# Values of a woven block in three visits to the banks instead of four, and two blocks' stores issued later from six output tiles

## Chip, cores and metric

The kernel runs on one core of one Trainium2 chip. Its metric is the device time of one execution in microseconds (us). A core has a matmul engine (TensorE, in profile rows PE, its weight loads PEld), VectorE (DVE), ScalarE (ACT), GpSimd (POOL) and SyncE (SP), which only issues transfers. Each takes its instructions in program order and waits at an instruction until the semaphores that it needs are there.

## What is computed

Attention inside chunks of 64 tokens, then a feed-forward layer with a squared ReLU:

```python
# q, k, v: (8, 8, 576, 64), chunks of 64
scores = scale * np.matmul(q_c, k_c.transpose(0, 1, 2, 4, 3))
attn = np.exp(scores) / np.sum(np.exp(scores), axis=-1, keepdims=True)
out = np.matmul(attn, v_c)
# x: (4608, 512), w_in: (512, 2048), w_out: (2048, 512)
h = np.maximum(x @ w_in, 0.0)
return (h * h @ w_out).astype(np.float32)
```

(The reference also subtracts each row's maximum before the exponential and adds 1e-9 to the sum.)

## The kernel before

The 4608 tokens are 18 groups of 256 (four chunks each), and 9 blocks of two groups. Groups 14 and 15, which are block 7, are put together from the last chunk of every batch entry ("rest"); their loads take more and smaller transfers.

**Attention of a group.** q and k are loaded by SP, cast to bf16 (`C`, lines 283 and 286, on GpSimd or ScalarE) and transposed by SP as a DMA (`TD`, line 292; the first groups by PE). `scores` (PE, line 315) writes 32 matmuls of 64x64 to a PSUM tile of two banks, `ps_att`; ScalarE takes the exponential into a tile `e` (line 326). `values` (PE, line 342) multiplies `e` with v. v has a column of ones, so each head pair's output of 64 columns has the row sum as its 65th. For each of the two token tiles `t` of a group there is one visit to the bank: 4 head pairs x 4 = 16 matmuls of 65 columns. After a visit `out_of_x` has VectorE take the reciprocals of the sums (line 276) and multiply (line 277) into a tile `x`. `transpose_x` (`XT`) turns `x` into `xT`, in the woven part from block 5 on by an SP DMA (line 366).

**Feed-forward.** Blocks 0 to 3 go through `ffn_in` (line 410) and then their output product. From block 4 on, both products are done in seven part products each in place of eight, by sums of quarters. The x sums (`x_sums`, on VectorE through line 444) have to be there before a block's first product (line 487, `quad_product`). Outputs are summed into tiles `o_sb` and stored by GpSimd (`store`, line 635).

**The woven part.** From block 4 on the order is written by hand. Each block `j` has 16 slots; in each there stand in-products of block `j` (`quad_step`), a piece of the output products of block `j - 1` (line 606), and what `at(j, slot, ...)` puts there. A slot such as 3.5 stands after the in-products of slot 4 and before its output products. For the attention of block `j + 1`:

```python
S0, V0, V1, X0 = ((1.5, 3.5), (4.5, 7.5), (6, 9.5), (10.5, 11)) if j == QUADS else (
    (0.5, 7), (2,8), (3.5, 9.5), (3.5, 11.5)) if is_whole(blocks[j + 1][0]) else (
    (3.5, 9), (5, 10), (7, 11.5), (11.5, 12))
```

These are the slots of scores (S0), of the first and second value visit (V0, V1) and of `XT` (X0), for the block's two groups. The first line is for block 5, the second for blocks 6 and 8, the third for block 7. All of these visits use the one `ps_att` tile, so each waits until the reader of the visit before is done. The loads of block `j + 2` are issued by SP in the same slots, one per slot, or two where that block is the "rest".

**Stores.** `summed_out` adds into an `o_sb` and calls `defer`, which in blocks 1 and 2 issues the store at once and later 8 slots later (`after`; `tock` counts the slots). The casts of groups 6 and 7 stand in GpSimd's queue between block 1's first and second store.

Of the kernel before, what the change touches and what calls it, by code (L numbers as in the profile page):

```python
# [11 lines left out]
FP32 = mybir.dt.float32  # L12
# [6 lines left out]
def kernel(  # L19
# [197 lines left out]
    def att_bank():  # L217
        if "out" in banks:
            return ps_att.tile([128, 1024], FP32, name="ps_att")
        state["att"] = state.get("att", 0) + 1  # L220
        if state["att"] % 2:
            return ps_att.tile([128, 1024], FP32, name="ps_att")
        return ps_att2.tile([128, 1024], FP32, name="ps_att2")
# [19 lines left out]
            copy(out=dst[:, t], in_=src[:, t])  # L243

    def qkT_tile():
        return att_pool.tile([128, 2, 2, n_hp, 128], BF16, name="qkT", bufs=4)

    def transpose_qk(g, q_pool, k_pool):
        if ("qkT", g) not in state:
# [18 lines left out]

    def e_tile():
        return att_pool.tile([128, 1024], BF16, name="e", bufs=3)  # L270

    def out_of_x(x, ps, n):

        o = ps[:, :, 0:n * (D + 1)].rearrange("p a (h d) -> p a h d", d=D + 1)
        rec = att_pool.tile([128, 2, n], FP32, name="rec", bufs=4)
        nc.vector.reciprocal(out=rec, in_=o[:, :, :, D])
        nc.vector.tensor_tensor(  # L277
            out=x, in0=o[:, :, :, 0:D], in1=rec.to_broadcast([128, 2, n, D]), op=ALU.mult)

    def cast_qk(g, copies):  # L280
        qkb = att_pool.tile([128, 2, 2 * H * D], BF16, name="qkb", bufs=2)
# [43 lines left out]
            s_in = ps.rearrange("p (b i q) -> p b q i", i=2, q=CH // 2)  # L325
        nc.scalar.activation(out=e_out, in_=s_in, func=AF.Exp, scale=scale)  # L326

    def values(g, tiles=(0, 1)):
        e = state["e", g]
        veb = v_even[g % NV].bitcast(BF16)  # L330
        vob = [v_odd[odd_tile[g, c] % NO].bitcast(BF16) for c in range(4)]
        if 0 in tiles:
            state["x", g] = att_pool.tile([128, 2, n_hp, 2, D], BF16, name="x", bufs=3)
        x = state["x", g]
        for t in tiles:
            ps = att_bank().rearrange("p (a f) -> p a f", a=2)
            for hp in range(n_hp):
                for a in range(2):
                    for p in range(2):
                        c = p ^ a  # L340
                        vb = vob[2 * t + p] if a else veb[:, t]
                        nc.tensor.matmul(  # L342
                            out=ps[64 * p:64 * p + 64, a, hp * (D + 1):(hp + 1) * (D + 1)],
                            lhsT=e[64 * c:64 * c + 64, a, hp, t, :],
                            rhs=vb[64 * c:64 * c + 64, hp, 1::2],
                            start=True, stop=True)
            out_of_x(x[:, t].rearrange("p h a d -> p a h d"), ps, n_hp)

    def transpose_x_early(g, t):
        psb = ps_ffn.tile([128, 512], FP32, name="ps_ffn").bitcast(BF16)  # L350
# [122 lines left out]
    def after(n, f):  # L473
        later.append((state["clock"] + n, f))
# [83 lines left out]
    def ffn_out(j):  # L558
# [82 lines left out]
                    in_=o_sb[:, t * HD:(t + 1) * HD])  # L641

        def o_tile():
            return ffn_pool.tile([128, n_tt * HD], FP32, name="o_sb", bufs=4)

        def summed_out(name, s, half, col):
            o = o_tile()
# [2 lines left out]
            defer(lambda: store(nc.gpsimd, o, half, col))  # L650

        def defer(f):
            if "out" in banks:
                    after(8, f)
            else:
                f()

        A, BC = 0, 1
        s1 = kept()
# [56 lines left out]
    def ffn_out_by_ft(j):  # L716

        n_tt = BT // 128
        o_ps = [ps_ffn.tile([128, d_model], FP32, name="ps_ffn") for _ in range(n_tt)]

        def mm(tt, ft):
            nc.tensor.matmul(  # L722
                out=o_ps[tt],
                lhsT=g_piece(j, tt // 2, ft // HF, ft % HF // 4)[
                    :, ft % 4, tt % 2 * 128:tt % 2 * 128 + 128],
                rhs=w_out_bf[:, ft, :],
                start=(ft == 0), stop=(ft == n_ft - 1))


        for ft in range(n_ft - 4):  # L730
            for tt in range(n_tt - 1 if ft == 0 else n_tt):
                mm(tt, ft)
                if ft == 1 and tt == n_tt - 2:
                    mm(n_tt - 1, 0)
            yield
        for tt in range(n_tt):
            for ft in range(n_ft - 4, n_ft):
                mm(tt, ft)
            o_sb = ffn_pool.tile([128, d_model], FP32, name="o_sb", bufs=4)
            nc.scalar.copy(out=o_sb, in_=o_ps[tt])  # L740
            b, s0 = chunks[blocks[j][tt // 2]][0]
            t0 = b * S + s0 + tt % 2 * 128
            nc.gpsimd.dma_start(out=out[t0:t0 + 128, :], in_=o_sb)
            yield
# [6 lines left out]
        for g in grps:  # L751
            yield from v_pieces(g)

    SC, AV, XT = scores, values, transpose_x
    TD = transpose_qk_dma

    def TE(g):
# [17 lines left out]
            copies = nc.gpsimd.tensor_copy, nc.gpsimd.tensor_copy  # L775
        cast_qk(g, copies)

    def AV0(g):
        values(g, [0])

    def AV1(g):
        values(g, [1])

    HT = BT // 2
    go(pieces([0, 1]))
# [37 lines left out]
    for j in range(QUADS):  # L823
        grps, nxt, far = blocks[j], blocks[j + 1], blocks[j + 2]
        plan = {}

        def at(slot, f, *x):
            plan.setdefault(slot, []).append((f, x))

        if j == 0:  # L830
            loads, go_slots = pieces(far), range(17)
            at(28, summed(b11_p_b21, b11, b21))
            for slot, f in ((24, TA), (27, SC), (29, AV), (31, XT)):
                at(slot, f, nxt[0])
            at(31, TQ, nxt[1])
            at(31, summed(b22_m_b21, b22, b21, ALU.subtract))
            phases = [first_ffn_in, ffn_out_by_ft(0)]
        elif j == 1:
            loads, go_slots = itertools.chain(*map(qk_pieces, far)), range(26, 48)
            for slot, f in ((1, TK), (4, SC), (7, AV), (12, XT)):  # L840
                at(slot, f, grps[1])
            for i, g in enumerate(nxt):
                for slot, f in ((16 + 4 * i, C), (21 + 4 * i, TD), (36 + i, SC), (38 + 2 * i, AV),
                                (41 + 2 * i, XT)):
                    at(slot, f, g)
            for i, g in enumerate(far):
                at(36 + 4 * i, C, g)
                at(42 + 3 * i, TD, g)
            at(2, summed(b12_p_b21, b12, b21))
            at(12, summed(b11_m_b12, b11, b12, ALU.subtract))  # L850
            at(20, summed(b12_p_b22, b12, b22))
            out_j = ffn_out(1)
            for i in (20, 27, 29, 31):
                at(i, lambda: next(out_j)())
            phases = [ffn_in(1, [(0, 256, FT_ORDER), (256, 256, FT_ORDER)]), out_j]
        else:
            out_j = ffn_out(j)
            for i in (14, 15):
                at(i, lambda: next(out_j)())
            phases = [ffn_in(j, [(0, BT, range(n_ft))])]  # L860
            if j == 2:
                loads, go_slots = itertools.chain(*map(v_pieces, nxt), pieces(far)), [
                    *range(16), *range(27, 36)]
                slots = {SC: (8, 7), AV: (10, 12), XT: (11, 14), C: (21, 26), TD: (29, 29)}
                for f in (C, TD):
                    for i, g in enumerate(far):
                        at(slots[f][i], f, g)
                phases.append(out_j)
            else:
                loads, go_slots = pieces(far), range(16)  # L870
                slots = {SC: (2, 4), AV: (7, 13), XT: (14, 15)}
            for f in (SC, AV, XT):
                for i, g in enumerate(nxt):
                    at(slots[f][i], f, g)
            if j == 2:
                for i, f in enumerate((summed(a21_p_a22, a21, a22),
                                       summed(a12_m_a21, a12, a21, ALU.subtract),
                                       summed(a11_p_a21, a11, a21))):
                    at(1 + 2 * i, f)
        slot = 0  # L880
        for phase in phases:
            for _ in phase:
                if slot in go_slots:
                    for f in loads:
                        f()
                        break
                for f, x in plan.get(slot, []):
                    f(*x)
                slot += 1
        assert all(x < slot for x in plan), (j, slot, sorted(plan))  # L890
        if j < QUADS - 1:
            go(loads)
# [19 lines left out]
    for j in range(QUADS, n_blk):  # L912
# [25 lines left out]
            plan.setdefault(("out", 16 * (j - QUADS) + s), []).append(outs[j - 1])  # L938

        if j + 1 < n_blk:  # L940
            S0, V0, V1, X0 = ((1.5, 3.5), (4.5, 7.5), (6, 9.5), (10.5, 11)) if j == QUADS else (
                (0.5, 7), (2,8), (3.5, 9.5), (3.5, 11.5)) if is_whole(blocks[j + 1][0]) else (
                (3.5, 9), (5, 10), (7, 11.5), (11.5, 12))
            for i, g in enumerate(blocks[j + 1]):
                at(j, S0[i], SC, g)
                at(j, V0[i], AV0, g)
                at(j, V1[i], AV1, g)
                at(j, X0[i], XT, g)
            for i, s in enumerate((13.5, 15, 17.5, 18)):
                at(j, s, x_sums, j + 1, i)  # L950
# [65 lines left out]
```

## Time and profile before

| | us |
|---|---|
| median of 3 runs | 287.72 |
| the runs | 284.68, 287.72, 289.44 |
| the profiled execution, device time | 285.11 |
| its span from first to last instruction | 283.2 |
| mean granted TensorE clock in it | 0.997 |

The page of the profile gives busy time by engine, the costliest groups of instructions, and the chain of work that ended last: from the last instruction back, at each step to what released it. Rows of a group give its line, engine, operation and tiles, its count, then busy time and the mean of one in ns. Some that matter here:

```profile
L410 PE MATMUL ps_ffn<-xT,w_in_bf 128*128 128x512 bf16 (+1 forms) x328 | 58.7, 333 | 0.3 <-DVE xT L376 0.2
L487 PE MATMUL ps_ffn<-qk_st,w_in_bf 128*128 128x256 bf16 x240 | 35.4, 273 | 1.8 <-DVE qk_st L444 1.7
L277 DVE TENSOR_TENSOR x<-ps_att,rec 128x512 bf16<-128x512 f32 x36 | 24.9, 692 | 1.2
L326 ACT ACTIVATE e<-ps_att 128x1024 bf16<-128x1024 f32 x18 | 18.4, 1024 | 12.7 <-PE ps_att L315 12.7
out_dram<-o_sb POOLq DMA_DIRECT2D x31, 256.0 KB, 3.9
```

The mean of one matmul is its time in the pipeline, of which several lie over one another; what a matmul takes of PE is the distance to the next one's start. The last row is a group of transfers: issued by GpSimd, 31 times, at most 256 KB each, 3.9 us from issue to landing in the median. By stretches, the DMA engines are busy throughout until about 211 us (a share near 1), then loads end.

### The profile page before, as it was taken

What the parts mean: (1) busy time and instruction counts of PE and PEld (TensorE: products, weight loads), DVE (VectorE), ACT (ScalarE), POOL (GpSimd) and SP (SyncE); (2) the same over time, 40 slices, a digit from 0 to 9 for tenths busy, and PEclk for the clock granted to TensorE, in tenths of its full rate; (3) what the DMA queues carried; (4) which work ended last, traced back from release to release, by engine and by line L of the source; (5) the groups of instructions that cost most, each with busy time, mean ns of one, the idle gap of its engine ahead of it and who ended that gap; (6) DMA issues with size and microseconds to landing.
All of it is one profiled execution on the core that took longest, in us unless ns stands there. A gap on an engine that the chain in (4) does not pass through costs nothing.

```text
span 283.2 us, 7888 instructions
## 1 busy us (share of the span) xinstructions
PE 266.0 (94%) x3255; PEld 202.9 (72%) x3258; DVE 199.2 (70%) x360; ACT 162.5 (57%) x292; POOL 92.6 (33%) x123
## 2 busy tenths in 40 slices
PE   1999999999998999997999999899999999999994
PEld 1774454778773468445888788688888888888783
DVE  1266615899648592388989998489879877984842
ACT  1537705786446764875666775476657664656330
POOL 2037834150242002132025425432543322431612
PEclk9999999999999999999999999999999999999998
DMA  7999999999998999999999899599996320120312
GB/s 199 239 299 362 374 331 248 317 215 178 264 218 231 234 212 237 269 247 195 271 241 189 224 197 223 121 254 258 229 180 175 74 73 6 80 71 0 93 58 111
DMA packets 139699, 56.61 MB, mean 200 GB/s; under 512 B 108496, under 2 KB 135376, under 8 KB 139664
## 3 DMA queue, kind: packets, MB, share of 16 engines
q1 hardware_dynamic: 136656, 46.81, 75.4%
q0 software_dynamic: 2864, 9.18, 9.5%
q8 instruction: 25, 0.41, 0.6%
q10 hardware_dynamic: 144, 0.13, 0.1%
q14 instruction: 10, 0.08, 0.1%
HBM read 36.70 MB, written 9.44 MB: 163 GB/s over the span
## 4 chain that ended last, share of the span: by engine, by line
PE 78%; DMA 9%; DVE 7%; ACT 2%; issue 1%; POOL 0%; SPq 0%; DVEq 0%; ACTq 0%
PE ps_ffn L487 20%; PE ps_out L606 19%; PE ps_ffn L410 14%; PE ps_ffn L606 11%; PE ps_ffn L722 5%; DMA qk_st<-in_k_dram 4%; DMA xT<-x 3%; PE ps_att L315 3%; DMA qkT<-qkb 2%; PE ps_att L342 2%; DVE x L277 2%; DVE gT L428 2%; PE ps_ffn L267 1%; PE ps_ffn L234 1%; DVE relu L495 1%
## 5 line engine op out<-in xcount | busy, mean ns | idle before, releaser
L410 PE MATMUL ps_ffn<-xT,w_in_bf 128*128 128x512 bf16 (+1 forms) x328 | 58.7, 333 | 0.3 <-DVE xT L376 0.2
L606 PEld LDWEIGHTS <-w_st 128*128 128x128 bf16 x512 | 49.2, 98 | 7.9 <-DVE w_st L444 1.2
L428 DVE TENSOR_TENSOR gT<-relu 128x256 bf16<-128x256 bf16 (+2 forms) x69 | 34.8, 532 | 21.4 <-ACT relu L421 21.0
L495 DVE CUSTOM_DVE_ANT_0 relu<-ps_ffn,w_st 128x512 f32<-128x512 f32 x60 | 39.2, 684 | 13.2 <-PE ps_ffn L487 11.9
L421 ACT ACTIVATE relu<-ps_ffn 128x256 bf16<-128x256 f32 (+2 forms) x82 | 39.8, 503 | 13.0 <-PE ps_ffn L410 11.7
L410 PEld LDWEIGHTS <-w_in_bf 128*128 128x128 bf16 x328 | 30.8, 98 | 21.6 <-DVE xT L376 0.4
L487 PE MATMUL ps_ffn<-qk_st,w_in_bf 128*128 128x256 bf16 x240 | 35.4, 273 | 1.8 <-DVE qk_st L444 1.7
L635 POOL DMA_DIRECT2D out_dram<-o_sb x27 | 19.8, 732 | 50.3 <-DVE o_sb L444 49.4
L487 PEld LDWEIGHTS <-w_in_bf 128*128 128x128 bf16 x320 | 30.5, 98 | 6.3 <-DVE qk_st L444 2.6
L606 PEld LDWEIGHTS <-gT 128*128 128x128 bf16 x296 | 28.6, 98 | 3.6
L606 PE MATMUL ps_out<-w_out_bf,w_st 128*128 128x256 bf16 x240 | 30.8, 273 | 0.0
L529 ACT ACTIVATE w_st<-ps_ffn 128x512 f32<-128x512 f32 x20 | 11.9, 596 | 28.4 <-PE ps_ffn L487 28.4
L277 DVE TENSOR_TENSOR x<-ps_att,rec 128x512 bf16<-128x512 f32 x36 | 24.9, 692 | 1.2
L326 ACT ACTIVATE e<-ps_att 128x1024 bf16<-128x1024 f32 x18 | 18.4, 1024 | 12.7 <-PE ps_att L315 12.7
L487 PEld LDWEIGHTS <-qk_st 128*128 128x128 bf16 x240 | 22.7, 98 | 2.9
L506 POOL TENSOR_TENSOR qk_st<-relu 128x512 bf16<-128x512 f32 x10 | 10.3, 1034 | 43.3 <-DVE relu L495 43.3
L487 PE MATMUL ps_ffn<-xT,qk_st 128*128 128x256 bf16 x160 | 23.9, 273 | 0.0
L506 POOL TENSOR_TENSOR gT<-relu 128x512 bf16<-128x512 f32 x10 | 10.3, 1033 | 38.0 <-DVE relu L495 38.0
L283 POOL CAST qkb<-qk_st 128x1024 bf16<-128x1024 f32 x12 | 13.3, 1104 | 18.6 <-DMA qk_st<-in_q_dram 10.3
L606 PE MATMUL ps_ffn<-w_out_bf,w_st 128*128 128x256 bf16 x144 | 17.7, 273 | 0.4 <-DVE w_st L444 0.3
L504 ACT ACTIVATE gT<-relu 128x512 bf16<-128x512 f32 x28 | 17.7, 632 | 0.0
L444 DVE TENSOR_TENSOR w_st<-gT,w_st 128x1024 bf16<-128x1024 bf16 x26 | 17.0, 687 | 0.0
(83 smaller groups left out, 419.9 us busy)
## 6 DMA issues: line engine op xcount, KB each, us to landing
qk_st<-in_q_dram SPq DMA_DIRECT2D x16, 512.0 KB, 5.8
out_dram<-o_sb POOLq DMA_DIRECT2D x31, 256.0 KB, 3.9
qk_st<-in_k_dram SPq DMA_DIRECT2D x24, 256.0 KB, 5.6
ve_sb<-in_v_dram SPq DMA_DIRECT2D x32, 128.0 KB, 4.4
w_st<-in_moe_w_in_dram SPq DMA_DIRECT2D x8, 512.0 KB, 6.6
w_st<-in_moe_w_out_dram SPq DMA_DIRECT2D x8, 512.0 KB, 6.2
vo_sb<-in_v_dram SPq DMA_DIRECT2D x24, 128.0 KB, 4.1
qk_st<-in_k_dram SPq DMA_DIRECT2D x4, 512.0 KB, 6.7
```

The costliest lines, as they stand in the source:

```text
L277: nc.vector.tensor_tensor(out=x, in0=o[:, :, :, 0:D], in1=rec.to_broadcast([128, 2, n, D]), op=ALU.mult)
L326: nc.scalar.activation(out=e_out, in_=s_in, func=AF.Exp, scale=scale)
L410: nc.tensor.matmul(out=h[:, 0:n], lhsT=w_in_bf[:, dt, ft * 128:(ft + 1) * 128], rhs=xT[:, c // 128:(c + n) // 128, dt, :], start=(dt == 0) ...
L421: nc.scalar.activation(out=rl[:, 0:n], in_=h[:, 0:n], func=AF.Relu)
L428: nc.vector.tensor_tensor(out=dst, in0=src, in1=src, op=ALU.mult)
L444: nc.vector.tensor_tensor(out=out, in0=in0, in1=in1, op=op)
L487: nc.tensor.matmul(out=bank[:, f * GT:(f + 1) * GT], lhsT=a[:, dt, ft * 128:(ft + 1) * 128], rhs=b[:, :, dt, :], start=(first and f == 0 a ...
L495: nc.vector._custom_dve(TENSOR_ADD_SAT, out=out, in0=in0, in1=in1, s0=BIG, s1=0.0)
L504: engine.activation(out=dst, in_=r, func=AF.Square)
L506: engine.tensor_tensor(out=dst, in0=r, in1=r, op=ALU.mult)
L606: nc.tensor.matmul(out=out_ps, lhsT=lhsT, rhs=b[:, i, :], start=(first and i == 0 and (last or t == 0)), stop=(i == HF - 1), skip_group_ch ...
L635: dma.dma_start(out=out[t0:t0 + GT, col:col + HD].rearrange("(t p) d -> p t d", p=128), in_=o_sb.rearrange("p (t d) -> p t d", d=HD))
```

## The change

A visit no longer holds one token tile of one group. `values` takes a list of parts (group, tile, head pair), up to seven, whose columns (7 x 65 = 455 of a bank's 512) fit one bank on each side. The 16 parts of a block's two groups are cut into visits of 7, 7 and 2 (`AVB`). The second visit spans both groups, so it has two multiplies, one of 1 part and one of 6. In blocks 0 to 3 and the start a visit is one tile as before (`AV`). The slots of the woven part change with it. `qkT` has three buffers in place of four, `o_sb` six in place of four. The stores of block 1 are issued 12 slots later, those of block 2 ten; the slots of blocks 0 to 3 are counted for it.

```diff
-        return att_pool.tile([128, 2, 2, n_hp, 128], BF16, name="qkT", bufs=4)
+        return att_pool.tile([128, 2, 2, n_hp, 128], BF16, name="qkT", bufs=3)
...
-    def values(g, tiles=(0, 1)):
...
+    def values(parts):
+
+        ps = att_bank().rearrange("p (a f) -> p a f", a=2)
+        for n, (g, t, hp) in enumerate(parts):
+            if (t, hp) == (0, 0):
+                state["x", g] = att_pool.tile([128, 2, n_hp, 2, D], BF16, name="x", bufs=3)
+            e = state["e", g]
+            veb = v_even[g % NV].bitcast(BF16)
+            for a in range(2):
+                for p in range(2):
+                    c = p ^ a
+                    vb = v_odd[odd_tile[g, 2 * t + p] % NO].bitcast(BF16) if a else veb[:, t]
+                    nc.tensor.matmul(
+                        out=ps[64 * p:64 * p + 64, a, n * (D + 1):(n + 1) * (D + 1)],
+                        lhsT=e[64 * c:64 * c + 64, a, hp, t, :],
+                        rhs=vb[64 * c:64 * c + 64, hp, 1::2],
+                        start=True, stop=True)
+        o = ps[:, :, 0:len(parts) * (D + 1)].rearrange("p a (h d) -> p a h d", d=D + 1)
+        rec = att_pool.tile([128, 2, 7], FP32, name="rec", bufs=4)[:, :, 0:len(parts)]
+        nc.vector.reciprocal(out=rec, in_=o[:, :, :, D])
+        for g in sorted({z[0] for z in parts}):
+            n = [i for i, z in enumerate(parts) if z[0] == g]
+            n0, n1 = n[0], n[-1] + 1
+            u = n_hp * parts[n0][1] + parts[n0][2]
+            nc.vector.tensor_tensor(
+                out=state["x", g].rearrange("p t h a d -> p a (t h) d")[:, :, u:u + n1 - n0],
+                in0=o[:, :, n0:n1, 0:D],
+                in1=rec[:, :, n0:n1].to_broadcast([128, 2, n1 - n0, D]), op=ALU.mult)
...
-            return ffn_pool.tile([128, n_tt * HD], FP32, name="o_sb", bufs=4)
+            return ffn_pool.tile([128, n_tt * HD], FP32, name="o_sb", bufs=6)
...
         def defer(f):
-            if "out" in banks:
-                    after(8, f)
-            else:
-                f()
+            after((12, 10)[j - 1] if j < 3 else 8, f)
...
+    def AVB(j, i):
+        cuts = (0, 7, 14, 16)
+        both = [z for g in blocks[j] for z in parts_of(g)]
+        values(both[cuts[i]:cuts[i + 1]])
...
                 slot += 1
+                tock()
...
-            S0, V0, V1, X0 = ((1.5, 3.5), (4.5, 7.5), (6, 9.5), (10.5, 11)) if j == QUADS else (
-                (0.5, 7), (2,8), (3.5, 9.5), (3.5, 11.5)) if is_whole(blocks[j + 1][0]) else (
-                (3.5, 9), (5, 10), (7, 11.5), (11.5, 12))
+            S0, V0, X0 = ((1.5, 3.5), (6, 7.5, 9.5), (10.5, 11)) if j == QUADS else (
+                (0.5, 2.5), (4.5, 8, 9.5), (9, 11.5)) if is_whole(blocks[j + 1][0]) else (
+                (3.5, 5.5), (8, 10, 11.5), (11.5, 12))
             for i, g in enumerate(blocks[j + 1]):
                 at(j, S0[i], SC, g)
-                at(j, V0[i], AV0, g)
-                at(j, V1[i], AV1, g)
+            for i in range(3):
+                at(j, V0[i], AVB, j + 1, i)
+            for i, g in enumerate(blocks[j + 1]):
                 at(j, X0[i], XT, g)
```

More of the change, by code (lines that the diff above doesn't have):

```diff
@@ L270, in e_tile @@
         return att_pool.tile([128, 1024], BF16, name="e", bufs=3)
[L272 to L278, printed above, removed]
     def cast_qk(g, copies):
@@ L326, in scores @@
         nc.scalar.activation(out=e_out, in_=s_in, func=AF.Exp, scale=scale)
-    def values(g, tiles=(0, 1)):
[L329 to L347, printed above, removed]
+    def values(parts):
[25 more added lines that the diff above has]
+                in1=rec[:, :, n0:n1].to_broadcast([128, 2, n1 - n0, D]), op=ALU.mult)
@@ L349, in transpose_x_early, with parts_of @@
+    def parts_of(g, tiles=(0, 1)):
+        return [(g, t, hp) for t in tiles for hp in range(n_hp)]
     def transpose_x_early(g, t):
@@ L738, in ffn_out_by_ft @@
                 mm(tt, ft)
-            o_sb = ffn_pool.tile([128, d_model], FP32, name="o_sb", bufs=4)
+            o_sb = ffn_pool.tile([128, d_model], FP32, name="o_sb", bufs=6)
             nc.scalar.copy(out=o_sb, in_=o_ps[tt])
@@ L752, in pieces @@
             yield from v_pieces(g)
-    SC, AV, XT = scores, values, transpose_x
+    SC, XT = scores, transpose_x
     TD = transpose_qk_dma
@@ L776, in C, with AV @@
         cast_qk(g, copies)
[L778 to L782, printed above, removed]
+    def AV(g, tiles=(0, 1)):
+        for t in tiles:
+            values(parts_of(g, [t]))
+    def AVB(j, i):
+        cuts = (0, 7, 14, 16)
+        both = [z for g in blocks[j] for z in parts_of(g)]
+        values(both[cuts[i]:cuts[i + 1]])
     HT = BT // 2
```

## The prediction

> **What bounds the kernel now.** I read the page's busy line and chain first:
>
> ```profile
> PE 266.0 (94%) x3255; PEld 202.9 (72%) x3258; DVE 199.2 (70%) x360; ACT 162.5 (57%) x292; POOL 92.6 (33%) x123
> PE 78%; DMA 9%; DVE 7%; ACT 2%; issue 1%; POOL 0%; SPq 0%; DVEq 0%; ACTq 0%
> ```
>
> TensorE bounds it: only 17.2 us of the 283.2 us span are not PE time, and some 11 us of these lie in the start (0 to 20 us, 6.5) and the tail (after 266 us, 4.3), which the change does not touch. So the next view is one of windows, for the four stretches in which attention of the next block is woven in; two of them:
>
> ```profile
> 156.00:183.50 27.50, 26.17 (x344) 22.06 (x344) 22.71 (x42) 17.44 (x31) 12.15 (x13) 1.00 0.89 191
> 210.90:238.00 27.10, 27.09 (x355) 23.15 (x356) 22.65 (x41) 17.02 (x30) 6.94 (x8) 1.00 0.40 99
> ```
>
> The columns are the length, then PE, weight load, DVE, ACT and POOL busy, granted clock, DMA share, GB/s. The second stretch is full of matmuls; the first has 1.33 us without one. Where, the chain of waits in order of time says (start, length, what):
>
> ```profile
> 84.81 6.41 DMA qkT<-qkb
> 91.26 0.45 PE ps_att L315 x32
> ...
> 179.87 3.19 DMA xT<-x
> 183.08 0.44 DVE qk_st L444
> 183.56 1.05 PE ps_ffn L487 x8
> ...
> 205.58 0.69 DVE x L277
> 206.30 4.10 DMA xT<-x
> 210.91 1.05 PE ps_ffn L487 x8
> ```
>
> Three times PE stands for a DMA transpose: at 91.26 for the scores of group 7, and at 183.56 and 210.91 for the first product of blocks 6 and 7, whose x sums (DVE, L444) wait for xT. A chain row of 8 matmuls of 256 columns takes 0.87 us, 0.109 each. The last matmuls before 183.56 are 8 from 181.13 on, so PE was free at 182.00 and stood 1.56; before 210.91 the same count gives 0.46. Those are the waits that a PE saving can run into.
>
> **Fewer visits.** What a visit of the values to the bank costs, the PE timeline shows:
>
> ```profile
> 143.76 1.04 PE L606 MATMUL ps_out<-w_out_bf,w_st 128*128 128x256 bf16 x8
> 144.73 0.22 PE L342 MATMUL ps_att<-ve_sb,e 64*64 64x65 bf16 x2
> ...
> 144.99 0.72 PE L487 MATMUL ps_ffn<-qk_st,w_in_bf 128*128 128x256 bf16 x5
> ```
>
> 143.76 + 8 x 0.109 = 144.63, and the visit begins at 144.73: 0.095 to get in. Its 16 small matmuls start within about 0.13 us and the next large one comes at 144.99, some 0.095 more than their own spacing. So 0.19 us of each visit is entry and exit; the matmuls (about 10 ns each) stay the same. Four woven blocks go from 16 visits to 12: 4 x 0.19 = 0.75 us off PE, if nothing else waits.
>
> On DVE the four reciprocals (L276, 198 ns) become three, and four multiplies of 512 elements (L277, 692 ns) become four of 896, 128, 768 and 256. Taking the 198 ns of the tiny one as the fixed part, an element costs (692 - 198)/504, about 1 ns: 1.08, 0.31, 0.95 and 0.44 us, together as before. But the first two visits hold the bank longer: 0.2 + 1.08 = 1.3 us and 0.2 + 0.31 + 0.95 = 1.46, against 0.9. The tightest place is block 5's, where 12 matmuls (1.31 us) stand between the first and the second visit: results at about 144.85, multiply done at 146.2, second visit due at 146.16. I put 0.1 us there, bounds 0 and 0.6 (one more DVE instruction queued ahead). The other gaps hold 20 to 52 matmuls (2.2 us or more): nothing, or 0.3 with the same instruction ahead.
>
> **Scores earlier.** For blocks 6 and 8 the second group's scores move from slot 7 to 2.5, for block 7 from 9 to 5.5. Their input comes by an SP transpose (L292). For group 13:
>
> ```profile
> L292 SPq DMA_TRANSPOSE qkT<-qkb x1: 2715/2715/2715, 156.9 to 156.9; - x1
> ...
> DMA to landing us min/median/max: 6.3/6.3/6.3
> ```
>
> It lands at 156.87 + 6.3 = 163.2. In the new order these scores follow 8 output products (from 159.99) and 4 matmuls: 159.99 + 12 x 0.109 + 0.09 = 161.4. PE will stand 1.8 us there, a wait that before does not have, with everything of PE behind it. What is late next? PE reaches the start of block 6 at 182.00 + 1.8 - 0.19 - 0.19 (two visits saved) = 183.4, and that start is set by the transpose anyway: 179.87 + 3.19 + 0.46 = 183.5. So the new wait takes the place of the old one and costs about 0.0, provided that the second xT transpose of block 6 still issues at 179.87. On SP, the first one moves behind ten loads (slot 3.5 to 9); the loads are the same, so the second stays where it is if the first need not wait at its new place. The ten loads were issued from 167.80 to 175.3; without the transpose ahead, which ran from 166.28, SP is through with them at about 173.7. The x is done after the second visit (170.02 before, so about 171.8, plus 0.5 and the reciprocal and short multiply, 0.5 to 0.9): 172.8 to 173.2. Half a microsecond of margin.
>
> For block 8 the group's transpose (issued 211.49, 4.2 to landing) is there at 215.7 and its scores are due 20 matmuls behind the first group's (213.63 + 0.38 + 2.18 + 0.09, less 0.4 from the next part: 215.9): nothing, bounds 0 and 0.3. For block 7, the transpose issued at 185.75 has landed long before 193: nothing.
>
> **Block 7's x.** Its last visit now holds 2 of 16 parts: 0.25 us less multiply, 0.08 less on PE, 0.23 us earlier by the visit already saved, less some delay of the longer multiply ahead. I take x 0.4 us earlier (bounds 0 and 0.75), so the 206.30 transpose and the 210.91 start move 0.4: that is what block 7's saving of 0.19 and its wait of 0.46 allow.
>
> **Stores and tiles.** Eight stores are issued 12 or 10 slots later in the program, but in GpSimd's queue only one changes its place: block 1's first, which passes the casts of groups 6 and 7. The other seven have the same neighbours and the same semaphore to wait for.
>
> ```profile
> 73.71 0.71 POOL L635 DMA_DIRECT2D out_dram<-o_sb  x1 [9.42 <-DVE o_sb L444]
> 84.72 2.14 POOL L635 DMA_DIRECT2D out_dram<-o_sb  x3
> ```
>
> So x1 and x3 become x4 from 84.72. The casts between them waited for loads (1.1 to 2.1 us each), not for the store. The page's queue 0 has 2864 packets, 9.18 MB and 9.5% of 16 engines' span: 3.2 KB and 150 ns a packet. So a store of 256 KB is 80 packets, about 0.8 us of the 16 engines. Without it the loads of group 7 may land up to 0.8 us earlier, with it the transpose at 84.81 may land 0.8 later: ends -0.8 and +0.8 at the wait before 91.26, and I take 0, as the traffic only moves. qkT with three buffers: a transpose waits for scores three groups back, which are over a block old; nothing. Six output tiles: nothing waited for one.
>
> **Sum.** Start of block 6: 0 (-0.1 to +0.4), and what blocks 5 and 6 saved is gone in it. Block 7: -0.4. Block 8: -0.19, with 0 for its scores. Stores 0. Together -0.6; on the profiled execution's own time of 285.11 (span 283.2 and 1.9 around it) that is 284.5. The other runs gave 284.68, 287.72 and 289.44; the median of the four is 286.4, and 286.4 - 0.6 = 285.8.
>
> **Rivals.**
> - *The scores' wait is not absorbed* (slower). If x of group 12 is later than SP's arrival at 173.7, SP stands, and every load and the second transpose behind it slip by as much; a slip of 1.56 keeps the old wait as well. Price 1.8 - 0.19 = 1.6 at block 6, in all +1.0: 286.1 profiled, 287.4 beside the runs. For it: the margin is only 0.5. Against: it must be overrun by 1.5 to count fully. 0.2.
> - *The fourth store delays the transpose* (slower). With three stores in flight the transpose at 84.81 took 6.4 us, the one for group 13, with one (issued 156.79), 6.3, so rows do not settle it. Price 0.8 at 91.26, in all +0.2: 285.3 profiled, 286.6 beside the runs. The Trainium skill, "DMA: Bandwidth & Descriptors", section "SWDGE vs HWDGE vs iDMA", says that DMAs from GpSimd and from SP sit in different queues of each engine, which it serves in turn; by it a fourth store takes its share from the transpose. 0.12.
> - *More is won.* Group 7's loads land 0.8 earlier, the transpose too, and SP carries that through to 183.5: -0.6 - 0.8 = -1.4, at most -2.3 (0.75 of visits, 1.1 that PE waits for the transpose before 91.26, 0.46 before 210.91): 282.8 to 283.7 profiled. 0.13.
> - *It does nothing*, PE's saving being taken up by DMA everywhere: 0, 285.1. That lies within 0.6 of the forecast and shares its chance of 0.5; 0.05 is left for what I do not see.
>
> **Numbers.** The likeliest is 285.8. The range goes from the fastest time shown less 1.8, inside the larger gain (282.9), to the slowest less 0.4, inside the forecast and the second rival (289.0); the runs' own scatter of 4.8 us is most of it. A change under 2% (5.8 us) cannot be told from none here, and no case above reaches it; what I leave beyond is for unseen causes and scatter: faster 0.1, same 0.83, slower 0.07.
>
> **What would show it.** Right: 12 value visits after 136 us; a wait of 1.5 to 2 us before L315's scores near 161, and none or little before block 6's first product at 183.4 to 183.7; four stores in a row from about 84; the 210.91 start a little earlier relative to 183.5. Wrong: a gap before a value visit of more than 0.5 us, both waits (161 and 183) present, or the transpose before 91 landing much later. The sum would be overturned if the loads' pace on SP changed, since they, not PE, set the start of block 6.

## The result, and the profile after

The changed kernel takes 296.44 us in the median of six runs (295.03 to 298.07), the kernel before 287.39 in the runs beside it (284.68 to 294.36). The ratio is 1.034, with a 95% interval of 1.028 to 1.041: slower by some 9 us. The ratios here and below leave out runs over 1.5% above the fastest of the same kernel, so they differ a little from the quotients of the medians. The forecast was 285.8, with a range up to 289.0. The profiled execution took 296.31 us, its span 294.4, at a mean granted TensorE clock of 0.979 (before 0.997).

The busy line and the chain's shares, from the page of the changed kernel:

```profile
PE 270.2 (92%) x3258; PEld 205.2 (70%) x3258; DVE 197.6 (67%) x356; ACT 163.2 (55%) x292; POOL 93.1 (32%) x123
PE 67%; DMA 12%; DVE 8%; SPq 7%; ACT 3%; issue 1%; POOL 1%; ACTq 0%
```

The span grew by 11.2 us and PE's busy time by 4.2 only, although PE has fewer visits to make. So most of the time was not lost on PE's own work (and a part of the 4.2 is the half clock, see below). The chain says SPq 7% where it said 0%, and DMA 12% where it said 9%; that is a hint and no more, for the chain splits differently from one execution to the next. What PE waits for, by line, releaser, total, times and longest (us), first before:

```profile
PE ps_att L371 <- DVE x L277: 2.1, 2, 1.6
PE ps_ffn L487 <- DVE qk_st L444: 1.7, 2, 1.4
PE ps_att L315 <- DMA qkT<-qkb: 1.1, 1, 1.1
```

and after (L307 is the scores, L374 the PE transposes of `x`, L490 the first products):

```profile
PE ps_att L307 <- DMA qkT<-qkb: 7.0, 3, 3.5
PE ps_att L374 <- DVE x L344: 2.5, 1, 2.5
PE ps_ffn L490 <- DVE qk_st L447: 1.2, 2, 1.1
```

The row that grew is the scores' wait for the DMA transposes of q and k, 1.1 to 7.0 us. Two of them in the chain of waits, in order of time:

```profile
85.88 8.12 DMA qkT<-qkb
94.05 0.45 PE ps_att L307 x32
...
163.74 7.84 DMA qkT<-qkb
171.62 0.45 PE ps_att L307 x32
```

The first is the transpose for group 7, which before was issued at 84.81 and took 6.41; the second is the one for group 13, before 6.3 us from 156.9. Both start later and take longer. And PE pays for its waits a second time, by the view of windows (length, then PE, weight load, DVE, ACT and POOL busy, granted clock, DMA share, GB/s):

```profile
72.00:100.00 28.00, 24.49 (x365) 15.14 (x364) 14.11 (x29) 15.00 (x22) 6.96 (x8) 0.94 1.04 222
94.40:97.81 3.41, 3.41 (x51) 1.38 (x40) 0.43 (x1) 2.48 (x3) 0.00 (x0) 0.50 1.07 220
135.40:138.81 3.41, 3.41 (x22) 2.22 (x19) 1.53 (x3) 1.76 (x3) 0.22 (x1) 0.50 0.82 180
156.00:183.50 27.50, 23.82 (x312) 19.65 (x312) 22.42 (x40) 15.41 (x28) 10.68 (x12) 0.94 1.00 191
172.90:176.31 3.41, 3.41 (x44) 2.24 (x42) 2.88 (x5) 1.26 (x3) 1.73 (x2) 0.50 1.08 204
183.50:211.00 27.50, 27.50 (x338) 23.90 (x337) 22.06 (x39) 17.57 (x32) 12.67 (x15) 1.00 0.86 197
```

Directly behind the wait that ends at 94.05 the clock is granted at half for 3.41 us; so it is from 135.4 and from 172.9, behind waits of 2.6 and 3.7 us. None of this was in the windows of before, all at 1.00 between 60 and 238 us.

How far the same matmul is later than before, at points of the order that both kernels share, worked out from the two traces: 0.4 us at 62, 1.2 at 74, 4.2 at 93.4 (a wait of 2.93 where it was 1.23, and the half clock), 6.5 at 132 (a wait of 2.64 where it was 1.81, and the half clock), 11.5 at 168 (a wait of 3.66 before group 13's scores, new, and the half clock), 10.0 at the start of block 6, 11.1 at 224. The growth ends where the loads end. (A wait is here, as in the prediction, the distance between the starts of two matmuls less the spacing of the first; the views count from its modelled end and give 0.16 to 0.17 us less.)

The row of the `qkT` transposes themselves, first before, then after (SP's issue of one in ns, least, median and most; then from issue to landing):

```profile
L292 SPq DMA_TRANSPOSE qkT<-qkb x14: 1617/2020/3817, 65.8 to 211.5; - x14
DMA to landing us min/median/max: 3.8/4.4/6.4
```

```profile
L284 SPq DMA_TRANSPOSE qkT<-qkb x14: 1328/2852/4108, 67.0 to 222.5; - x14
DMA to landing us min/median/max: 4.3/4.9/8.1
```

The change issues the same 14 transposes of the same size in the same places, and yet the median issue went from 2.02 to 2.85 us and even the quickest landing from 3.8 to 4.3. Queueing would move the median and the worst; a least time that rises points at the transfer itself. The sum of the 14 issues is 32.6 us before and 38.9 after. While SP issues a transpose it issues none of the loads behind it.

### The profile page after: what moved, and what is told of

Same layout as the page of the kernel before. It is cut to its first block, busy times and chain, and to the rows that moved or that the text cites. A ratio compares the mean times of both kernels' runs of the same rounds, so it can differ in the third digit from the quotient of the medians.

```text
span 294.4 us, 7869 instructions
## 1 busy us (share of the span) xinstructions
PE 270.2 (92%) x3258; PEld 205.2 (70%) x3258; DVE 197.6 (67%) x356; ACT 163.2 (55%) x292; POOL 93.1 (32%) x123
## 4 chain that ended last, share of the span: by engine, by line
PE 67%; DMA 12%; DVE 8%; SPq 7%; ACT 3%; issue 1%; POOL 1%; ACTq 0%
PE ps_out L609 19%; PE ps_ffn L490 19%; PE ps_ffn L413 11%; PE ps_ffn L609 9%; DMA qkT<-qkb 5%; PE ps_ffn L722 5%; DVE gT L431 4%; DMA w_st<-in_moe_w_in_dram 3%; DMA qk_st<-in_k_dram 2%; SPq L136 2%; PE ps_att L332 2%; PE ps_att L307 2%; SPq L181 2%; DMA xT<-x 2%; SPq L177 1%
## 5 line engine op out<-in xcount | busy, mean ns | idle before, releaser
L413 PE MATMUL ps_ffn<-xT,w_in_bf 128*128 128x512 bf16 (+1 forms) x328 | 61.3, 341 | 1.0 <-POOL w_in_bf L197 0.6
L431 DVE TENSOR_TENSOR gT<-relu 128x256 bf16<-128x256 bf16 (+2 forms) x69 | 34.2, 525 | 25.9 <-ACT relu L424 25.2
L413 PEld LDWEIGHTS <-w_in_bf 128*128 128x128 bf16 x328 | 31.1, 99 | 23.9 <-issue 1.8
L490 PE MATMUL ps_ffn<-qk_st,w_in_bf 128*128 128x256 bf16 x240 | 35.6, 273 | 1.2 <-DVE qk_st L447 1.2
L490 PEld LDWEIGHTS <-w_in_bf 128*128 128x128 bf16 x320 | 31.1, 98 | 5.6 <-DVE qk_st L447 1.8
L609 PE MATMUL ps_out<-w_out_bf,w_st 128*128 128x256 bf16 x240 | 31.4, 276 | 0.0
L344 DVE TENSOR_TENSOR x<-ps_att,rec 128x512 bf16<-128x512 f32 (+4 forms) x36 | 24.5, 690 | 1.1
L490 PEld LDWEIGHTS <-qk_st 128*128 128x128 bf16 x240 | 23.1, 98 | 2.9
L490 PE MATMUL ps_ffn<-xT,qk_st 128*128 128x256 bf16 x160 | 24.0, 276 | 0.0
```

Source lines behind the costliest of these rows:

```text
L344: nc.vector.tensor_tensor(out=state["x", g].rearrange("p t h a d -> p a (t h) d")[:, :, u:u + n1 - n0], in0=o[:, :, n0:n1, 0:D], in1=rec[: ...
L413: nc.tensor.matmul(out=h[:, 0:n], lhsT=w_in_bf[:, dt, ft * 128:(ft + 1) * 128], rhs=xT[:, c // 128:(c + n) // 128, dt, :], start=(dt == 0) ...
L431: nc.vector.tensor_tensor(out=dst, in0=src, in1=src, op=ALU.mult)
L490: nc.tensor.matmul(out=bank[:, f * GT:(f + 1) * GT], lhsT=a[:, dt, ft * 128:(ft + 1) * 128], rhs=b[:, :, dt, :], start=(first and f == 0 a ...
L609: nc.tensor.matmul(out=out_ps, lhsT=lhsT, rhs=b[:, i, :], start=(first and i == 0 and (last or t == 0)), stop=(i == HF - 1), skip_group_ch ...
```

## The experiments

Each was run beside the kernel before on the same chip; ratios are to it, with 95% intervals. The first four split the change as the prediction had seen it.

**Scores back to their slot.** The changed kernel, with the second scores of blocks 6 and 8 where they were:

```diff
-                (0.5, 2.5), (4.5, 8, 9.5), (9, 11.5)) if is_whole(blocks[j + 1][0]) else (
+                (0.5, 7), (4.5, 8, 9.5), (9, 11.5)) if is_whole(blocks[j + 1][0]) else (
```

> The changed kernel with one thing put back: the second group's scores of blocks 6 and 8 stand at slot 7 again, as before, not at 2.5. Theory S (these scores now stand ahead of the landing of their transpose; PE idles 3.66 us at 171.6, which also brings 3.41 us at half clock, and 0.95 at 227.6; 1.5 of it is given back at block 6): about 296.4 - 3.7 - 1.7 + 1.5 - 1.0 = 291.5, no wait over 1 us before these scores, mean clock about 0.985, and the 1.5 us wait before block 6 is back. Theory Q (the store moved behind the casts sets it, through the transpose that lands at 94.0): 296.4 within 1. Theory C (the waits come and go by chance with the DMA traffic): 296.4 within 2, with waits at other places.

Measured: 297.04 us, ratio 1.035 (1.028 to 1.042). Nothing came back. The early scores, the first place that the prediction doubted, are not the cause by themselves.

**Stores back.** The changed kernel, with the stores of blocks 1 and 2 issued at once:

```diff
         def defer(f):
-            after((12, 10)[j - 1] if j < 3 else 8, f)
+            if "out" in banks:
+                after(8, f)
+            else:
+                f()
```

> The changed kernel with the stores of blocks 1 and 2 issued at once, as before (buffers as changed). Theory Q (four stores in a row delay the transpose of group 7, which lands 1.7 us later after its cast than before, and the 2.9 us wait of PE then brings 3.41 us at half clock): the wait before the scores near 92 is about 1.2 us again, no half clock there, about 296.4 - 1.7 - 1.6 = 293. Theory S (the early scores set it): 296.4 within 1, wait near 94 still about 3. Theory C: waits at other places, 296.4 within 2.

Measured: 295.22 us, ratio 1.030 (1.023 to 1.037). Not the cause by itself either.

**Both back.** The two edits together; what is left of the change is the three visits with their slots, block 7's earlier scores, and the tiles.

> The changed kernel with both put back, scores of blocks 6 and 8 at slot 7 and stores of blocks 1 and 2 at once: what is left is the three visits and the buffers. Theories S and Q add: about 288, or a few tenths under the kernel before (the 0.75 us of four visits, less what the transposes of xT take back), mean clock 0.99 or more. S alone or Q alone: 291.5 or 293. Theory C: anything from 287 to 297. A rival V (the longer visits themselves cost, by waits of PE for the bank): over 290 with waits before the value visits.

Measured: 293.92 us (290.63 to 299.93), ratio 1.022 (1.013 to 1.031). Most of the loss is in what the prediction had costed at a gain of 0.75 us or at nothing.

**Stores and tile counts alone.** The kernel before, with the later stores and the buffer counts of the change:

```diff
-        return att_pool.tile([128, 2, 2, n_hp, 128], BF16, name="qkT", bufs=4)
+        return att_pool.tile([128, 2, 2, n_hp, 128], BF16, name="qkT", bufs=3)
...
-            return ffn_pool.tile([128, n_tt * HD], FP32, name="o_sb", bufs=4)
+            return ffn_pool.tile([128, n_tt * HD], FP32, name="o_sb", bufs=6)
...
+            after((12, 10)[j - 1] if j < 3 else 8, f)
...
+                tock()
```

> The kernel before with the store part of the change alone (stores 12 and 10 slots later, six output tiles, three qkT buffers). Theory Q: 287.4 + 3.3 = 290.7, a wait of about 3 us near 94 and half clock after it. Theory S: 287.4 within 1, the wait near 91 about 1.2. Theory C: within the scatter of the kernel before.

Measured: 286.64 us, ratio 0.998 (0.994 to 1.003). This part of the forecast, 0, holds.

Beside the three visits, the three kernels that stayed slow share one thing that the fourth lacks. The change makes the tile of the reciprocals larger, from [128, 2, 4] to [128, 2, 7] fp32. By the two programs' allocations, a buffer goes from 32 bytes of a partition to 56, placed every 64, and four of them from 128 to 256. Every tile behind it (`xT`, `qkb`, and the next pool's `o_sb`) moves by 128 bytes against a multiple of 512. (The dropped `qkT` buffer is 4096 bytes and changes nothing in that.) `qkb` begins at byte 211456 before, a multiple of 512, and at 207488 after, 128 past one; and `qkb` is what the transposes read. The second four runs test that.

**The change with the addresses put back.** The only edit is the width of a tile whose extra columns nothing uses:

```diff
-        rec = att_pool.tile([128, 2, 7], FP32, name="rec", bufs=4)[:, :, 0:len(parts)]
+        rec = att_pool.tile([128, 2, 20], FP32, name="rec", bufs=4)[:, :, 0:len(parts)]
```

> The changed kernel with the tile of reciprocals widened once more, from [128, 2, 7] to [128, 2, 20] (used as before), so that the tiles behind it in SBUF (xT, qkb, o_sb) start at multiples of 512 bytes again, as in the kernel before; in the changed kernel they start 128 bytes past one. Theory L (that offset slows the qkT transposes, which read qkb, and the stores, which read o_sb, and PE waits for them): issue times of the qkT transposes back near 2 us, the PE waits before scores near 75 and 94 at most about 1, no half clock there: 288 or less, at most the wait of some 1.8 before the early scores of block 6, as forecast. Theory V (the three visits and their slots cost): 296 within 1. Theory C (chance): 293 to 298.

Measured: 289.49 us, ratio 0.999 (0.995 to 1.003). The whole loss is gone. The transposes, in its profiled execution:

```profile
L284 SPq DMA_TRANSPOSE qkT<-qkb x14: 1602/2232/4257, 68.0 to 218.7; - x14
DMA to landing us min/median/max: 3.8/4.4/6.9
```

The least and the median landing are those of before again.

**The addresses alone.** The kernel before, with four visits and all its slots, and a wider tile of which it uses four columns:

```diff
-        rec = att_pool.tile([128, 2, n], FP32, name="rec", bufs=4)
+        rec = att_pool.tile([128, 2, 7], FP32, name="rec", bufs=4)[:, :, 0:n]
```

> The kernel before with the tile of reciprocals widened from [128, 2, 4] to [128, 2, 7] and nothing else: xT, qkb and o_sb move to 128 bytes past a multiple of 512. Theory L: slower like the third experiment, 292 to 295, with longer qkT transposes and PE waits before scores. Theory V: 287 within 1.

Measured: 296.09 us, ratio 1.022 (1.016 to 1.027). No instruction differs but in addresses and in the length of a row of the reciprocals' tile, and 6.4 us are lost.

**Which tile.** First `o_sb` alone, by 128 bytes ahead of it:

```diff
+    ffn_pool.tile([128, 32], FP32, name="pad")
```

> The kernel before with 128 bytes of padding ahead of o_sb alone: the stores read from 128 past a multiple of 512, the transposes do not. Theory L by way of the stores (their 4096-byte packets took 160 ns in the median before and 179 after): most of the loss is here, 290 or more, also through transposes that run beside stores. L by way of the transposes' source: 287 within 1, store packets near 180 ns.

Measured: 289.62 us, ratio 1.000 (0.996 to 1.004). The stores' packets took 171 ns in the median in place of 160, and no time came of it.

Then `xT` and `qkb` shifted and `o_sb` not (the wide `rec`, and 384 bytes ahead of `o_sb`):

```diff
+    ffn_pool.tile([128, 96], FP32, name="pad")
...
-        rec = att_pool.tile([128, 2, n], FP32, name="rec", bufs=4)
+        rec = att_pool.tile([128, 2, 7], FP32, name="rec", bufs=4)[:, :, 0:n]
```

> The kernel before with the wider tile of reciprocals and 384 bytes of padding ahead of o_sb: xT and qkb stand 128 past a multiple of 512, o_sb does not. L by way of the transposes: 290 to 294, qkT transposes longer, store packets at 160 ns. L by way of the stores: 287 within 1.

Measured: 295.72 us, ratio 1.022 (1.018 to 1.027). So it is `xT` or `qkb`. The next takes `qkb` alone, by 128 bytes between the two, again with 384 ahead of `o_sb` so that it stays:

```diff
+    ffn_pool.tile([128, 96], FP32, name="pad")
...
+        if "pad" not in state:
+            state["pad"] = att_pool.tile([128, 32], FP32, name="pad2", bufs=1)
```

> The kernel before with 128 bytes of padding between xT and qkb and 384 behind qkb: qkb alone stands 128 past a multiple of 512; xT and o_sb stand as before. Theory Q1 (the source of the qkT transposes matters): the loss of the two tiles together, 2.2%, is here: 1.015 to 1.025 of the kernel before, qkT transposes issue in 2.5 us or more where they took about 2. Theory X (xT, which the xT transposes write, matters): 1.00 within 0.5%.

Measured: 295.34 us, ratio 1.025 (1.020 to 1.030). It is `qkb`. And the same with 256 bytes in both places (64 columns in place of 32 and 96):

> The kernel before with qkb alone moved by 256 bytes: 256 past a multiple of 512. If only the boundary of 256 counts, the transposes are as quick as before and the time is 1.00 within 0.5% of the kernel before; if 512 counts, 1.01 to 1.025. The Trainium skill, DMA: Bandwidth & Descriptors, section How a descriptor splits into AXI transactions, has a transaction start at a multiple of 256 bytes, so by it there is no loss here.

Measured: 288.33 us, ratio 1.000 (0.996 to 1.004). The transposes of the two, 128 and then 256 bytes past a multiple of 512:

```profile
L296 SPq DMA_TRANSPOSE qkT<-qkb x14: 1345/2828/3929, 66.2 to 220.9; - x14
DMA to landing us min/median/max: 4.3/5.4/7.7
```

```profile
L296 SPq DMA_TRANSPOSE qkT<-qkb x14: 1317/2200/3592, 67.5 to 216.2; - x14
DMA to landing us min/median/max: 3.8/4.7/7.2
```

The 14 issues sum to 37.9 us with 128 and to 33.7 with 256. Over all profiles of this study, the next two included, the eight with `qkb` at 128 past have a least landing of 4.2 to 4.5 us and a median issue of 2.71 to 2.98; the six with it at 0 or 256 past have 3.7 to 3.9 and 2.02 to 2.28. So of the offsets tried (0, 128 and 256) 256 is as good as 0: a multiple of 256 bytes is enough, and one of 512 is not needed. The Trainium skill, "DMA: Bandwidth & Descriptors", section "How a descriptor splits into AXI transactions", says that a transaction begins at a multiple of 256 bytes, so that a descriptor which begins between two of them fetches bytes it does not need. The traces agree: 4.3 us at 128 past, 3.8 at 256. That this is how a transpose reads is not something that a trace here shows.

**Is it the half clock?** The rival to slow transposes as the direct cost was that PE's half clock behind each wait makes the loss. The changed kernel, with PE kept at work through the three waits by matmuls whose results are overwritten:

```diff
+    def fill(ps):
+        for _ in range(36):
+            nc.tensor.matmul(out=ps[:, 0:128], lhsT=ident, rhs=ident, start=True, stop=True)
...
+        if g in (7, 13):
+            fill(ps)
...
+        if g == 8:
+            fill(bank)
```

> The changed kernel with 36 matmuls of 128 columns (about 2 us; they write to the bank that the next real ones overwrite) put before three PE waits: those before the scores of groups 7 and 13 (2.9 and 3.7 us) and before the transposes of group 8's x (2.6). The data that PE waits for come no sooner. Theory H (a wait of over 2.3 us or so brings 3.41 us at half clock, about 1.7 us lost each): the waits proper stay, the granted clock stays at 1.0 there, mean clock 0.99 or more, time 296.4 - 3 x 1.7 = 291.3, at most 1 more where a wait is shorter than the filling. Without H: 296 or slower.

Measured: 297.08 us, ratio 1.032 (1.025 to 1.039). The mean granted clock of the profiled execution is 1.000, and yet nothing came back. Its windows and PE's timeline (in brackets the idle time ahead and its releaser; L313 is the scores):

```profile
72.00:100.00 28.00, 26.76 (x413) 17.66 (x412) 15.74 (x33) 15.81 (x23) 6.96 (x8) 1.00 0.95 211
```

```profile
144.75 0.45 PE L313 MATMUL ps_att<-qkT 64*64 64x64 bf16 x32 [1.39 <-DMA qkT<-qkb]
...
225.09 0.45 PE L313 MATMUL ps_att<-qkT 64*64 64x64 bf16 x32 [1.88 <-DMA qkT<-qkb]
```

What PE gains from the clock it gives back at later scores, for groups that had not waited so long: 1.39 us at 144.75, 1.88 at 225.09. SP meanwhile issues the transposes at about the same times as in the changed kernel, the first of a pair at 138.4, 161.6, 190.5 and 218.7 us in place of 137.6, 160.0, 191.8 and 218.3. That fits a pace set by the transposes and the loads behind them, which a faster PE only meets sooner. Nor is the half clock needed for a loss: the profile of the change with both back has none between 60 and 230 us (1.00 throughout), and took 293.57 us.

**A version with the large attention tiles and `o_sb` on multiples of 512.** The changed kernel with its scores at the old slot, a `rec` of 16 columns, and 128 bytes ahead of `qkT`, so that `x`, `e` and `qkT` are moved too (they lie at 384 past a multiple in both kernels):

```diff
+    att_pool.tile([128, 32], FP32, name="pad", bufs=1)
...
-        rec = att_pool.tile([128, 2, 7], FP32, name="rec", bufs=4)[:, :, 0:len(parts)]
+        rec = att_pool.tile([128, 2, 16], FP32, name="rec", bufs=4)[:, :, 0:len(parts)]
...
-                (0.5, 2.5), (4.5, 8, 9.5), (9, 11.5)) if is_whole(blocks[j + 1][0]) else (
+                (0.5, 7), (4.5, 8, 9.5), (9, 11.5)) if is_whole(blocks[j + 1][0]) else (
```

> The changed kernel with the scores of blocks 6 and 8 at slot 7 and all tiles of the attention pool, also qkT, e and x, at multiples of 512 bytes (in both kernels qkT, e and x stood 384 past one). Theory L: at least the realigned kernel's 1.00; the early scores' wait of 2.3 us with half clock is gone, so 0.985 to 0.995 of the kernel before. If also the source of the xT transposes counts (x, 128 past a multiple of 256 in both kernels), these issue in under 1.2 us and land sooner, and the waits before blocks 6 and 7 (1.6 and 0.5) shrink: 0.98 to 0.99. If the early scores were free once the transposes are quick: 1.00.

Measured: 290.67 us, ratio 1.007 (1.004 to 1.011). The quickest transpose of `x` lands in 2.71 us in place of 3.03, but no time is won, and the wait before block 6, which early scores had absorbed, is back in its profiled execution (294.93 us, the longest of its runs):

```profile
191.69 0.84 PE L492 MATMUL ps_ffn<-qk_st,w_in_bf 128*128 128x256 bf16 x4 [2.85 <-DVE qk_st L449]
```

Which of its two differences from the aligned change costs the 0.7% was not tried. No version beat the kernel before.

## Why the prediction was wrong

**The step that failed** is the part "Stores and tiles", which ended "Six output tiles: nothing waited for one". It asked of each changed tile how many buffers it has and who waits for one. It never asked where the tiles behind it come to lie, and for the reciprocals' tile, whose new width is in the diff, it named no cost at all. That width alone costs 2.2% (6.4 us) on the kernel before, `qkb` alone 2.5% (6.9 us); with the old addresses the whole change is worth nothing (0.999). No rival had the mechanism: "unseen causes" got 0.07 on the slower side.

**What bounds the kernel** was read too much from PE's 94%. PE was indeed busy, but the prediction's own last sentence had the condition: the sum is overturned "if the loads' pace on SP changed". It did. SP's first transpose of each pair of groups is issued 1.2 us later than before at 66, 2.2 at 80 and 109, 5.0 at 133, 6.7 at 153, 9.2 at 183 and 9.5 at 209. Filling PE's waits won nothing, which points the same way from the other side.

Point by point, the rest of the sum:

- **Fewer visits, 0.75 us of PE.** The 12 visits are there, and the multiply of 7 parts takes 1.09 us (forecast 1.08), that of 2 parts 0.42 (0.44). No time of it is seen: the aligned change measures 0.999 (0.995 to 1.003), an interval of 2.4 us in which 0.6 could hide.
- **Scores of group 13 wait and the wait before block 6 goes.** Right in kind: the old wait of 1.56 us at 183.56 is gone in the profile after (block 6 starts at 193.54 without one, and the shift falls from 11.5 to 10.0 us there). Its size was 3.66 us in place of 1.8, mostly since the transpose took 7.84 us in place of 6.3; it was issued 6.9 us later, but PE too was 6.7 us late. In the profiled execution of the aligned change it is 2.26 us, close to the 1.8.
- **Block 7's x 0.4 earlier.** Its last multiply is 0.1 earlier against the start of block 6, and its transpose takes 4.6 us in place of 4.1, so the start of block 7 lost 0.5 more there.
- **Stores.** Four in a row, as forecast, and worth nothing when nothing else is changed (0.998). (A store of 256 KB is 64 packets of 4096 bytes, 0.64 us of the 16 engines at the 160 ns of their median, not the 80 packets and 0.8 us of the prediction.) In the timeline of the changed kernel's GpSimd:

```profile
85.79 2.85 POOL L638 DMA_DIRECT2D out_dram<-o_sb  x4
```

- **The transpose before 91 "landing much later"** was named as a sign that the forecast is wrong. It was the first sign in the trace: 94.00 in place of 91.2.

**What stays open.** The change costs 3.4%, its addresses alone 2.2 to 2.5%. Taking back scores or stores alone gives 1.035 and 1.030, both together 1.022. That early scores and a fourth store cost something only where the transposes are slow would fit this, but the intervals (0.7 to 0.9 each way) overlap, and it is not shown. Nor is it shown which way the slow transposes cost the time. Over all profiles their 14 issues sum to 37.9 to 41.3 us with `qkb` at 128 past and to 32.2 to 33.7 otherwise, a difference of the size of the loss, but SP's longer issue and the later landing were not tried apart. The wait for group 8's `x`, 2.64 us after and 1.81 before, is also 2.65 in the profiled execution of the aligned change (292.28 us, above that kernel's median). It does not follow the addresses: its idle time is 2.5 us with the addresses alone changed, and 1.3 us both with `qkb` alone moved by 128 bytes and in the change with both back. What sets it was not tried.

## What to carry to other kernels

A tile's size is also an address for every tile behind it in its pool, and in the next pool. When a small tile grows, compare where the sources of DMA transposes lie in both programs before costing anything else; put small tiles last, or pad them, so that the large ones stay on multiples of 256 bytes (here 0 and 256 past a multiple of 512 were equally quick). And when one kind of transfer is slower at its least time, not only in its median, look at the transfer rather than at the queue.

## What the runs showed of the hardware

- A DMA transpose from SBUF to SBUF whose source lies 128 bytes past a multiple of 256 takes 4.2 to 4.5 us at the least in place of 3.7 to 3.9, and its issue on SP 2.7 to 3.0 us in the median in place of 2.0 to 2.3. The smaller transposes of `x`, whose source lies at 384 past a multiple of 512 in every run but the last, take 3.02 to 3.20 us at the least in those and 2.71 in the last, where it lies on a multiple. Plain stores from a tile at 128 past have packets of 171 to 187 ns in the median (seven profiles) in place of 159 to 160 (the other seven), without effect on the time where `o_sb` alone was moved (1.000).
- TensorE's granted clock falls to 0.50 for 3.41 us behind a wait of 2.6 to 3.7 us (from 94.4, 135.4 and 172.9 in the profile after). The length of the wait alone does not decide: one of 2.26 us did it in the aligned change and an idle time of 1.94 us with `qkb` at 256 past, while a wait of 2.41 us did not in the change with the stores back, nor an idle time of 2.52 us with the addresses alone changed. In every profile with more than one such stretch, their starts lie whole multiples of 3.41 us apart (in the profile after 41.0 and 37.5 us, 12 and 11 of them). So how a wait lies in a fixed raster of 3.41 us may count; no run here tests that. The Trainium skill, "TensorE: Matmul & The Clock Gate", section "Why this matters for your kernels", asks for no idle gap over about 3 us; here the measurement decides, and shorter gaps were enough, though not always. That filling the waits won no time (1.032 in place of 1.034) is the more useful half: here the half clock was not what set the pace.
